# Another order of the operations of chunks 7 and 8 in a fused attention and feed-forward kernel

## The chip, the cores and the metric

The kernel runs on one core of a Trainium2 chip. The metric is the device time of one execution in microseconds (us), the median over several runs. The core's engines are named as in the profile: PE (matrix products; PEld is its weight load), DVE, ACT, POOL and SP. DVE and ACT do elementwise work and read what PE leaves in PSUM; SP, ACT and POOL also issue the transfers (DMAs), each in the order of its own instructions.

## What is computed

Linear attention with cosine and sine weights, then a feed-forward layer with a Swish of its own slope for each column:

```python
q_p = phi(q, cos_w, sin_w)          # relu(x)*cos, relu(x)*sin, side by side
k_p = phi(k, cos_w, sin_w)
kv  = np.einsum('bhsf,bhsd->bhfd', k_p, v)
z   = np.sum(k_p, axis=2)
num = np.einsum('bhsf,bhfd->bhsd', q_p, kv)
den = np.einsum('bhsf,bhf->bhs', q_p, z)[..., None] + 1e-06
x   = (num / den) laid out as 4608 tokens x 512
h   = x @ w_in                      # 512 x 2048
out = (h * sigmoid(beta * h)) @ w_out   # 2048 x 512
```

Batch 8, 8 heads, 576 positions, 64 per head; inputs and output are float32, the products are done in bf16.

## The kernel before

The 4608 tokens are done in nine chunks of 512 (0 to 8). Each chunk's feed-forward part is two large products, and both are done in pairs with seven block products in place of eight (Strassen's scheme): DVE forms sums of input blocks, PE does seven products, and DVE and ACT put the results together in PSUM.

For chunk c there are eight pairs `h0` to `h7` (each gives two column blocks of h) and two pairs `ox` and `oy` of the output. A chunk has four token tiles of 128; pair `ox` makes tiles 0 and 2, pair `oy` tiles 1 and 3. The steps of a pair have one letter each, and `fast_ops` (L455) gives them:

- `1`, `5`, `6`, `2`, `7`, `3`, `4` are the seven products on PE, 2 matmuls each in an `h` pair and 8 in an `o` pair. The digit behind `1` is the PSUM bank of results "b", the digit behind `c` that of results "a".
- `c` (ACT, L471) copies the first product into bank a; `d` (ACT) or `D` (DVE), L475, keeps product 5 in a buffer in SBUF.
- `e` and `f` (DVE, L478) add that buffer to bank b, `e` after product 6 and ahead of 7, `f` after product 7 and ahead of 4. In an `o` pair `f` writes the right half of the second tile into an output buffer, and the kept product and PSUM are its inputs.
- `A` and `B` end the pair. In an `h` pair they are ACT's activation (L416) of bank a (after product 3) and bank b (after product 4). In an `o` pair `A` copies bank a, which is the whole first tile (L648), and `B` the left half of the second (L651), both on ACT; `X` and `Y` are the same copies on DVE, and `U`, `V` (L642) copy the halves of the first tile apart, on DVE.

`s` is one DVE sum of activations for the output products (L406), `t` one of the chunk's inputs (L446), `x` the division that ends the attention of three position blocks. Output buffers come from a pool of four and are taken in the order of the code; the buffers of `d` and `D` come from three names with two each, also in that order.

The order of all this is written out by hand: `ORDERS` holds a string of operations for each chunk, `7/` in the string of chunk 8 marks an operation that belongs to chunk 7, and the code issues them in this order. Each engine then runs its own share strictly in turn and waits where an input is not there yet.

Each finished tile, or half, is stored at once by `store` (L523). For the last chunk the issuing engine depends on the tile: both halves of tile 0 (the copy `oxA`) go by POOL, tiles 1 and 3 (pair `oy`) by SP for one half of the rows and by ACT for the other, tile 2 (`oxf` and `oxB`) by SP and POOL:

```python
own = (nc.sync if c < NTC - 1 else nc.gpsimd if tt == 0 else (nc.sync, nc.scalar if tt % 2 else nc.gpsimd)[hf])
```

In the last chunk's pair `oy` the second tile is stored in halves (`last`, in `o_pair`): the right half as part of `oyf`, the left half as part of `oyY`. So the ACT engine's instruction list holds, beside its copies, the store issues that belong to `oyU`, `oyf`, `oyV` and `oyY`.

Of the kernel before, what the change touches and what calls it, by code (L numbers as in the profile page):

```python
# [22 lines left out]
def kernel(  # L23
# [827 lines left out]
    def w_out_sum(kind):  # L851
# [73 lines left out]
            "oxB oy4 oyV oyY"),  # L925
    }

    pairs, parts = {}, {}
# [111 lines left out]
```

## Time and profile before

| | us |
|---|---|
| median of 3 runs | 274.17 (273.17 to 275.35) |
| the profiled execution: its own time | 273.7 |
| the profiled execution: span from the first instruction to the last | 271.6 |
| PE busy in the span | 261.2 |
| DVE busy | 229.9 |
| ACT busy | 196.6 |
| POOL busy | 36.2 |

The span is 2.1 us shorter than that execution's own time, and that execution was 0.5 us under the median. In the rows below the first column is the start in us from the span's start, the second the duration, then the engine, the line of the code, the operation, what it writes and reads, and how many instructions a row holds; square brackets give the idle time before it and what ended it. A queue that issues DMAs is marked by a q behind the engine's name (SPq, ACTq). A row with a share of busy time is an average over its stretch.

### The profile page before, as it was taken

How to read it: one execution, taken by the hardware profiler on the slowest of the kernel's cores; microseconds unless marked ns; L12 is line 12 of the kernel's file. 1: busy time of each engine (PE TensorE's matmuls, PEld its weight loads, DVE VectorE, ACT ScalarE, POOL GpSimd, SP SyncE). 2: the span in 40 equal slices, each digit the busy share in tenths (PEclk: the TensorE clock that was granted, in tenths of full speed). 3: DMA queues.
4: the chain of work that ended last, by engine and by line, in shares of the span. 5: the costliest groups of instructions: out<-in, count | busy, mean ns of one | idle time of the engine just before them, and what ended most of it. 6: DMA issues, size and time to landing. Idle time of an engine off the chain costs nothing.

```text
span 271.6 us, 9158 instructions
## 1 busy us (share of the span) xinstructions
PE 261.2 (96%) x3784; PEld 212.3 (78%) x3784; DVE 229.9 (85%) x599; ACT 196.6 (72%) x398; POOL 36.2 (13%) x34
## 2 busy tenths in 40 slices
PE   7699999999999999999999999999999999999991
PEld 6356545556888888888888888888888888888880
DVE  5989999999999998999988988898689879856931
ACT  5778677897788996895799668953993479628710
POOL 1444000000003304200042015000330000000002
PEclk9999999999999999999999999999999999999999
DMA  6999999999999999999698878119803241006005
GB/s 239 368 396 382 390 390 304 388 218 360 216 202 329 312 274 229 315 281 234 184 193 257 195 103 246 43 23 119 193 2 64 53 100 33 0 2 156 4 19 135
DMA packets 52441, 54.00 MB, mean 199 GB/s; under 512 B 31232, under 2 KB 31760, under 8 KB 52400
## 3 DMA queue, kind: packets, MB, share of 16 engines
q1 hardware_dynamic: 51904, 52.77, 70.6%
q8 instruction: 29, 0.48, 0.7%
q0 software_dynamic: 144, 0.39, 0.6%
q10 hardware_dynamic: 352, 0.27, 0.4%
q14 instruction: 12, 0.10, 0.1%
HBM read 36.71 MB, written 9.44 MB: 170 GB/s over the span
## 4 chain that ended last, share of the span: by engine, by line
PE 85%; DMA 9%; DVE 2%; issue 1%; ACT 1%; SPq 1%; POOL 0%; ACTq 0%; POOLq 0%
PE ps L611 36%; PE ps L502 32%; PE ps L386 7%; DMA raw_q<-in_q_dram 6%; PE ps L297 4%; DMA raw_k<-in_k_dram 3%; PE ps L276 3%; PE ps L534 3%; DVE xs L319 1%; SPq L79 1%; PE ps L235 0%; PE ps L356 0%; DVE win L115 0%; POOL out_dram L527 0%; DVE qb L193 0%
## 5 line engine op out<-in xcount | busy, mean ns | idle before, releaser
L416 ACT ACTIVATE g_t<-ps,beta 128x512 bf16<-128x512 f32 x112 | 71.3, 691 | 7.0 <-PE ps L502 6.3
L502 PE MATMUL ps<-w_stage 128*128 128x256 bf16 x336 | 56.3, 273 | 0.0
L611 PEld LDWEIGHTS <-S 128*128 128x128 bf16 x512 | 49.6, 98 | 6.4 <-issue 0.4
L502 PEld LDWEIGHTS <-w_stage 128*128 128x128 bf16 x448 | 43.8, 98 | 5.1
L478 DVE TENSOR_TENSOR ps<-ps,p 128x256 f32<-128x256 f32 x85 | 35.9, 429 | 8.4 <-PE ps L502 3.3
L611 PEld LDWEIGHTS <-g_t 128*128 128x128 bf16 x384 | 36.8, 98 | 4.8
L502 PE MATMUL ps<-xt,win 128*128 128x256 bf16 x224 | 39.7, 273 | 0.0
L502 PEld LDWEIGHTS <-win 128*128 128x128 bf16 x336 | 32.6, 98 | 3.9
L611 PE MATMUL ps<-wout,g_t 128*128 128x256 bf16 x256 | 32.4, 273 | 0.0
L471 ACT COPY ps<-ps 128x256 f32<-128x256 f32 x72 | 26.4, 372 | 6.9 <-PE ps L611 3.7
L611 PE MATMUL ps<-wout,S 128*128 128x256 bf16 x256 | 31.1, 273 | 0.0
L611 PE MATMUL ps<-T,S 128*128 128x256 bf16 x256 | 30.9, 273 | 0.2 <-issue 0.2
L223 POOL TENSOR_TENSOR qs<-qt,tanr 128x1152 bf16<-128x1152 bf16 x6 | 14.3, 2389 | 118.7 <-ACT o_sb L648 55.4
L386 PE MATMUL ps<-xt,win 128*128 128x512 bf16 (+1 forms) x156 | 28.5, 341 | 0.1
L406 DVE TENSOR_TENSOR S<-g_t 128x512 bf16<-128x512 bf16 x64 | 25.6, 417 | 1.7 <-ACT g_t L416 1.2
L394 ACT ACTIVATE g_t<-ps,beta 128x512 bf16<-128x512 f32 x32 | 21.1, 690 | 4.9 <-PE ps L386 4.7
L386 PEld LDWEIGHTS <-win 128*128 128x128 bf16 x156 | 15.0, 98 | 11.7 <-issue 0.2
L319 DVE TENSOR_TENSOR xs<-ps,rden 128x768 bf16<-128x768 f32 (+4 forms) x26 | 22.8, 884 | 0.8
L478 DVE TENSOR_TENSOR ps<-ps,u 128x256 f32<-128x256 f32 x43 | 18.5, 429 | 5.1 <-PE ps L502 2.4
L475 ACT COPY p<-ps 128x256 f32<-128x256 f32 x27 | 9.9, 376 | 15.9 <-PE ps L611 11.4
L502 PE MATMUL ps<-xt,w_stage 128*128 128x256 bf16 x112 | 20.7, 273 | 0.0
L502 PE MATMUL ps<-w_stage,win 128*128 128x256 bf16 x112 | 19.8, 273 | 0.0
(99 smaller groups left out, 385.8 us busy)
## 6 DMA issues: line engine op xcount, KB each, us to landing
out_dram<-o_sb SPq DMA_DIRECT2D x65, 128.0 KB, 3.3
raw_v<-in_v_dram SPq DMA_DIRECT2D x7, 1152.0 KB, 7.9
raw_k<-in_k_dram SPq DMA_DIRECT2D x7, 1152.0 KB, 10.9
raw_q<-in_q_dram SPq DMA_DIRECT2D x7, 1152.0 KB, 7.4
w_stage<-in_moe_w_in_dram SPq DMA_DIRECT2D x3, 1024.0 KB, 13.3
w_stage<-in_moe_w_out_dram SPq DMA_DIRECT2D x2, 1024.0 KB, 8.8
w_stage<-in_moe_w_out_dram SPq DMA_DIRECT2D x4, 512.0 KB, 12.0
raw_q<-in_q_dram SPq DMA_DIRECT2D x2, 576.0 KB, 4.7
```

The costliest lines, as they stand in the source:

```text
L223: return eng.tensor_tensor(dst.rearrange("q n (g p) -> q n g p", g=2), src.rearrange("q n (g p) -> q n g p", g=2), tanr[:, n0:n1].unsqueez ...
L297: nc.tensor.matmul(ps[cols, bank + jj, slot * E : (slot + 1) * E], lhsT=(qts[b % 2], qs_of(b))[cs][rows, jp, n, cols], rhs=kv[rows, g, jp, ...
L319: nc.vector.tensor_tensor(o.rearrange("q j n s d -> q j (n s) d"), nv[:, :, a:z, :, 0:D].rearrange("q j n s d -> q j (n s) d"), rden[:, :, ...
L386: nc.tensor.matmul(ps[:, h_bank(c, jt), i * 64 : (i + w) * 64], lhsT=win[jt // 4][:, mi, (jt % 4) * P : (jt % 4 + 1) * P], rhs=xt[:, i : i ...
L394: return nc.scalar.activation(gs[c, jt // 4][:, jt % 4], ps[:, h_bank(c, jt)], AF.Silu, scale=beta[:, jt : jt + 1])
L406: return nc.vector.tensor_tensor(o, l, r, op=op)
L416: return nc.scalar.activation(gs[c, jt // 4][:, jt % 4], bank, AF.Silu, scale=beta[:, jt : jt + 1])
L471: return nc.scalar.copy(at("a", 0), at("b", 0))
L475: return (nc.scalar.copy if eng == "act" else nc.vector.tensor_copy)(st["p5"], at("b", 1))
L478: nc.vector.tensor_tensor(dst, at("b", 0), st["p5"], op=ALU.add)
L502: nc.tensor.matmul(dst, lhsT=l[:, g], rhs=r[:, :, g * HP : (g + 1) * HP], start=start and g == 0, stop=g == 1, skip_group_check=True)
L611: nc.tensor.matmul(dst, lhsT=l(i), rhs=r[:, i], start=start and i == 0, stop=i == order[-1], skip_group_check=True)
```

## The change

Only the strings of chunks 6, 7 and 8 in `ORDERS` differ; no operation is added or left out, but four of them change their engine.

```diff
@@ chunk 6, end
-            "h7B s10 h6B oy10 N25 s12 oyc3 ox14 s13 s23 oy2 s22 oxc7 oy5 ox2"),
+            "h7B s10 h6B oy10 N25 s12 oyc3 ox14 s13 s21 s23 oy2 s22 oxc7 oy5 ox2"),
@@ chunk 7, beginning
-            "h212 6/s20 6/s42 6/oyD 6/ox5 6/s21 6/x2 6/t1 6/s33 6/ox6 6/oy6 h315 h111 6/s30 h15 6/oxd 6/oye h25 6/s32 "
+            "h212 6/s20 6/oyd 6/s42 6/ox5 6/x2 6/t1 6/s33 6/ox6 6/oy6 h111 h315 6/s30 6/s41 h15 6/oxd 6/oye 6/s32 6/s43 "
...
-            "6/s41 h016 6/s40 6/s43 h2d 6/oxe 6/oy7 6/oyf 6/oy3 h1D 6/oyA 6/t2 t1 6/ox3 h35 6/t3 h05 h0D h3D h2c3 6/oy4 "
-            "6/oxA 6/t4 h22 h1c7 h26 6/oyB h2e h16 h1e 6/ox7 h23 t3 h3c0 h17 h27 h12 h13 6/oxf h36 h1f h2f h14 6/ox4 "
+            "h25 6/s40 6/oy7 6/oxe h2d h016 6/oyf 6/oy3 6/t2 6/ox3 h35 t1 6/t3 6/oyA h05 h0D h2c3 6/oy4 h1d 6/oxA h3D "
+            "6/t4 h22 h1c7 h26 h16 6/oyY 6/ox7 h2e h1e h23 t3 h17 h3c0 h27 h13 6/oxf h12 h36 h1f h2f h14 6/ox4 h3e h24 "
...
@@ chunk 8, middle
-            "7/s41 h07 h37 h33 7/oyD 7/oxd 7/s40 h3f h2B 7/oy2 7/oxc2 7/ox6 7/oye 7/ox2 7/s32 h32 7/oy7 7/s43 h3A 7/oxe "
-            "7/ox7 7/ox3 7/oyf 7/oxf 7/ox4 7/oxB h0f h34 7/oxX h02 h510 h112 h04 h3B h15 h1c7 7/oy4 h1D h55 h03 h16 "
+            "7/s41 h37 h07 7/oy2 h33 7/oyD 7/oxd 7/s40 h3f h2B 7/oxc2 7/ox6 7/oye 7/ox2 7/s32 h32 7/oy7 h3A 7/s43 h34 "
+            "7/oxe 7/ox7 7/oxf 7/ox3 7/oyf 7/ox4 7/oxB h0f 7/oxX h02 h510 h112 h04 h3B h15 h1c7 7/oy4 h03 h1D h55 h16 "
...
@@ chunk 8, end
-            "s23 s22 ox5 oyc7 s40 oxd oy5 s33 oy2 s42 s43 oyd s41 ox6 oy6 oxe ox3 oyU ox7 oye oxf oy7 ox4 oyf oxA oy3 "
-            "oxB oy4 oyV oyY"),
+            "ox5 s23 s22 s40 oyc7 oy5 s33 oxd oy2 s42 s43 oyd s41 ox6 oy6 oxe ox3 oyU oye ox7 oxf oy7 ox4 oxA oyf oy3 "
+            "oy4 oxB oyV oyY"),
```

Seen engine by engine, these are all the differences.

- **ACT.** `oyd` of chunk 6, `h1d` of chunk 7 and `h2d` of chunk 8 come to ACT from DVE; `oyB` of chunk 6 goes to DVE as `oyY`. In chunk 8, `h0c5` goes ahead of `h2A`, and chunk 7's `oyB` ahead of `h0A`. At the end `oxA` goes ahead of the store that belongs to `oyf`.
- **DVE.** The same four operations leave or come. Some of the sums change places: `s21` and `s41` of chunk 6 come earlier, `s22` of chunk 7 later, `s21` of chunk 8 earlier and `s31` later. In chunk 7 `oxf` goes ahead of `oyf`, and `h7D` ahead of `s11`.
- **PE.** `h11` and `h31`, `h12` and `h13` of chunk 7 change places; `oy7` of chunk 6 goes ahead of `h01` of chunk 7. In chunk 8, `h05` goes behind `h23` and `h27`, `h37` ahead of `h07`, `h34` from behind chunk 7's `ox4` to ahead of its `ox7`, `h03` ahead of `h55`; chunk 7's `oy2` goes ahead of `h33`.
- **SP and POOL** have the same lists as before.

The end of ACT's list, as a difference (rows that begin with - stand before, with + now). L475 are `oxd` and `oyd`, L527 the issue of a store, L648 is `oxA`, L651 `oxB`:

```order
-L475 COPY p_5203<-ps 128x256
-L475 COPY u<-ps 128x256
-L527 DMA out_dram<-o_sb 64x256 x2
-L648 COPY o_sb<-ps 128x512
+L475 COPY p_5212<-ps 128x256
+L475 COPY u<-ps 128x256
+L527 DMA out_dram<-o_sb 64x256
+L648 COPY o_sb<-ps 128x512
+L527 DMA out_dram<-o_sb 64x256
 L651 COPY o_sb<-ps 128x256
 L527 DMA out_dram<-o_sb 64x256 x2
```

Before, two store issues (of `oyU` and of `oyf`) stood ahead of the copy `oxA`; now one does, and that of `oyf` comes after it.

ACT's list at the beginning of chunk 7, before, from `oyc3` and `oxc7` of chunk 6 on:

```order
214 L471 COPY ps<-ps 128x256 x2
215 L475 COPY p_4586<-ps 128x256
216 L475 COPY p_4597<-ps 128x256
217 L648 COPY o_sb<-ps 128x512
218 L471 COPY ps<-ps 128x256
219 L648 COPY o_sb<-ps 128x512
220 L471 COPY ps<-ps 128x256
221 L651 COPY o_sb<-ps 128x256
222 L471 COPY ps<-ps 128x256
```

and now:

```order
214 L471 COPY ps<-ps 128x256 x2
215 L475 COPY u<-ps 128x256
216 L475 COPY p_4587<-ps 128x256
217 L475 COPY p_4604<-ps 128x256
218 L648 COPY o_sb<-ps 128x512
219 L471 COPY ps<-ps 128x256
220 L475 COPY p_4648<-ps 128x256
221 L648 COPY o_sb<-ps 128x512
222 L471 COPY ps<-ps 128x256 x2
```

The new row 215 is `oyd`, the new row 220 is `h1d`, which stands between `h2c3` (219) and `oxA` (221) with `h1c7` behind that; the L651 copy `oyB` is gone from here.

DVE's list where chunk 7's output pairs end, before:

```order
486 L478 TENSOR_TENSOR ps<-ps,p_4934 128x256
487 L478 TENSOR_TENSOR o_sb<-ps,p_4932 128x256
488 L478 TENSOR_TENSOR o_sb<-ps,p_4934 128x256
489 L478 TENSOR_TENSOR ps<-ps,p_4911 128x256
490 L648 COPY o_sb<-ps 128x512
```

and now:

```order
483 L478 TENSOR_TENSOR ps<-ps,p_4942 128x256
484 L478 TENSOR_TENSOR o_sb<-ps,p_4942 128x256
485 L478 TENSOR_TENSOR o_sb<-ps,p_4940 128x256
486 L478 TENSOR_TENSOR ps<-ps,p_4911 128x256
487 L648 COPY o_sb<-ps 128x512
```

The rows are `oxe`, then before `oyf`, `oxf` and now `oxf`, `oyf` (each known by the kept product that it reads), then `h0f` of chunk 8 and `oxX`.

18 rows, old and new, of the table ORDERS are left out of this document.

## The prediction, made before the changed kernel was run

> **What bounds the kernel now.** I read the page first, then the table by stretches over the part that the change touches, then the order of time at the end, and last the transfers of the end. On the page the span and the engines' busy time stand:
>
> ```profile
> span 271.6 us, 9158 instructions
> PE 261.2 (96%) x3784; PEld 212.3 (78%) x3784; DVE 229.9 (85%) x599; ACT 196.6 (72%) x398; POOL 36.2 (13%) x34
> ```
>
> An average hides whether the changed part has gaps. By stretches (start and end, length, then PE, PEld, DVE, ACT and POOL busy, the granted clock, the DMAs):
>
> ```profile
> 188.00:202.00 14.00, 14.00 (x130) 12.54 (x129) 10.76 (x30) 11.92 (x26) 4.79 (x2) 1.00 0.63 107
> ...
> 244.00:258.00 14.00, 14.00 (x130) 12.55 (x129) 10.64 (x29) 11.08 (x24) 0.00 (x0) 1.00 0.34 77
> 258.00:263.00 5.00, 5.00 (x48) 4.48 (x47) 2.25 (x6) 0.37 (x1) 0.00 (x0) 1.00 0.11 26
> 263.00:265.90 2.90, 2.83 (x26) 2.28 (x24) 0.88 (x3) 0.86 (x2) 0.69 (x1) 1.00 0.18 45
> 265.90:271.60 5.70, 0.00 (x0) 0.00 (x0) 0.39 (x1) 0.00 (x0) 1.06 (x3) 0.91 0.54 138
> ```
>
> From 188 us on PE has no pause until its last product, at the full granted clock: 14.00 of 14.00 us, 5.00 of 5.00. So everything that the change moves inside chunks 6 to 8 can win nothing; it can only make PE wait. The last 5.7 us are another matter: PE is done and only copies, stores and landings are left. There the end is set, and this is how it goes, engine by engine:
>
> ```profile
> 260.43 2.78 PE L611 MATMUL ps<-wout,S 128*128 128x256 bf16 x24
> 263.05 1.04 PE L611 MATMUL ps<-T,g_t 128*128 128x256 bf16 x8
> 264.79 1.04 PE L611 MATMUL ps<-T,g_t 128*128 128x256 bf16 x8
> ...
> 262.37 0.43 DVE L478 TENSOR_TENSOR o_sb<-ps,p 128x256 f32<-128x256 f32 x1 [1.23 <-PE ps L611]
> 263.25 0.42 DVE L478 TENSOR_TENSOR o_sb<-ps,u 128x256 f32<-128x256 f32 x1 [0.45 <-PE ps L611]
> 264.99 0.42 DVE L642 COPY o_sb<-ps 128x256 f32<-128x256 f32 x1 [1.32 <-PE ps L611]
> 265.87 0.42 DVE L651 COPY o_sb<-ps 128x256 f32<-128x256 f32 x1 [0.45 <-PE ps L611]
> ...
> 263.70 0.50 ACTq L527 DMA_DIRECT2D out_dram<-o_sb  x1
> 264.32 0.59 ACT L648 COPY o_sb<-ps 128x512 f32<-128x512 f32 x1 [5.94 <-PE ps L611]
> 264.80 0.38 ACT L651 COPY o_sb<-ps 128x256 f32<-128x256 f32 x1
> ```
>
> The 24 matmuls from 260.43 are `ox3`, `ox7` and `oy7`, then come `ox4` (263.05), `oy3` and `oy4` (264.79). DVE does `oxf`, `oyf`, `oyV`, `oyY`, each as soon as its product is there. ACT does not: it stands idle for 5.94 us and starts `oxA` at 264.32, though `ox3` was complete after its 8 matmuls, at about 260.43 + 1.04 = 261.5. The row above tells why. ACT's list holds the issue of `oyf`'s store ahead of `oxA`; it waits for `oyf` (263.25 + 0.42 = 263.67) and occupies ACT's list from 263.70 to 264.20. The profile's chain of waits takes the same way, DVE, then ACT's issue, then the copies:
>
> ```profile
> 263.25 0.43 DVE o_sb L478
> ...
> 263.70 0.50 ACTq L527
> ...
> 264.80 0.39 ACT o_sb L651
> ```
>
> The stores follow, and they come in one heap:
>
> ```profile
> 265.20 0.47 SPq L527 DMA_DIRECT2D out_dram<-o_sb  x1
> 265.21 0.71 POOL L527 DMA_DIRECT2D out_dram<-o_sb  x1 [64.52 <-ACT o_sb L651]
> 265.45 0.47 ACTq L527 DMA_DIRECT2D out_dram<-o_sb  x1
> 265.76 0.55 SPq L527 DMA_DIRECT2D out_dram<-o_sb  x1
> 265.92 1.04 POOL L527 DMA_DIRECT2D out_dram<-o_sb  x2
> 266.32 0.49 ACTq L527 DMA_DIRECT2D out_dram<-o_sb  x1
> 266.40 0.94 SPq L527 DMA_DIRECT2D out_dram<-o_sb  x1
> ```
>
> **The end, worked out.** The stores' time from issue to landing (queue, count, KB each, median us): first the two pairs that are alone (`oyU`, `oyf`), then those of the heap, then the two last (`oyY`).
>
> ```profile
> out_dram<-o_sb SPq DMA_DIRECT2D x2, 64.0 KB, 1.9
> out_dram<-o_sb ACTq DMA_DIRECT2D x2, 64.0 KB, 2.2
> ...
> out_dram<-o_sb POOLq DMA_DIRECT2D x3, 128.0 KB, 3.6
> out_dram<-o_sb SPq DMA_DIRECT2D x1, 128.0 KB, 2.3
> ...
> out_dram<-o_sb ACTq DMA_DIRECT2D x1, 64.0 KB, 4.1
> out_dram<-o_sb SPq DMA_DIRECT2D x1, 64.0 KB, 4.2
> ```
>
> The last store is issued at 266.40 and lands 4.2 us later, at 270.6; the span ends 1.0 us after that, at 271.6. A 64 KB store that takes about 2 us alone takes twice that behind the heap: 640 KB (`oxA` 256, `oxB` 256, `oyV` 128) were issued in the 1.2 us ahead of it.
>
> With the change, step by step:
>
> - `oxA` starts when `ox3` is there: 261.5, and ends at 262.1 (0.59). POOL's two issues follow from 262.1 (0.71, then 0.53, half of the row with two), done by 263.4. Behind the copy in ACT's list stands `oyf`'s store, not due until 263.70: no cost.
> - `oxB` needs `ox4` (263.05 + 1.04 = 264.1) and ACT's free list (264.20, then the 0.12 to the next copy that the rows show now): 264.32 in place of 264.80. Its stores go at 264.7: SP's 0.5 us earlier, POOL's, which stands third in POOL's list, 1.7 us earlier (it is the second of the row from 265.92 now, at about 266.44).
> - `oyV` is bound to PE (264.99). SP's issue for it now waits for SP's issue for `oxB`; it comes at 265.44 in place of 265.76.
> - `oyY` is bound to PE too: 265.87 + 0.42, so both its issues go at 266.32, SP's 0.08 earlier than now.
>
> So the last landing is 266.32 + L, the end 1.0 later. L has no row of its own. Its lower end is the lone 1.9 to 2.2, its upper end the present 4.2. In proportion to what is in the way, with ACT's rows (2.2 alone, 4.1 behind 640 KB, so 1.9 for 640): only `oyV`'s 128 KB ahead gives 2.2 + 0.4 = 2.6; `oxB`'s 256 KB still in the way as well gives 2.2 + 1.1 = 3.3. `oxB`'s stores are issued 1.6 us ahead of `oyY`'s and SP's of that size landed in 2.3, so most of them is through: I take 2.6. The end is 266.32 + 2.6 + 1.0 = 269.9, **1.7 us** earlier. The bounds: 2.4 us (L 1.9), 1.0 us (L 3.3), 0.1 us (L 4.2).
>
> The Trainium skill, page "DMA: Bandwidth & Descriptors", section "Anatomy of one DMA — SWDGE (gpsimd) path", has a fit of 2.0 us plus the bytes over 436 GB/s for one DMA. As an estimate from that page, 64 KB would take 2.15 us and `oyY` would land as if alone, a gain of 2.1. The lone rows, 1.9 and 2.2, agree with it; the heap's 4.1 and 4.2 do not.
>
> **The moves inside chunks 6 to 8.** Three 0.42 us copies leave DVE and one comes; ACT gets three and loses one. Neither engine ends the kernel, so the sums cost nothing unless PE meets a late operand. The closest of these places are two. First ACT in chunk 7 (`h2c3`, `oxA`, `h1c7`) and PE's use of the last, `h16`, which is the third of the four matmuls (0.109 apart: 264.79 less 263.05 over 16):
>
> ```profile
> 215.40 0.36 ACT L471 COPY ps<-ps 128x256 f32<-128x256 f32 x1
> 215.66 0.59 ACT L648 COPY o_sb<-ps 128x512 f32<-128x512 f32 x1
> 216.29 0.36 ACT L471 COPY ps<-ps 128x256 f32<-128x256 f32 x1
> ...
> 216.98 0.60 PE L502 MATMUL ps<-w_stage 128*128 128x256 bf16 x4
> ```
>
> `h1d` in between pushes `oxA` and `h1c7` back by 0.26 (the step from the first row to the second) to 0.37. `h1c7` then ends between 216.9 and 217.0, `h16` is due at 217.2: 0.2 to 0.3 us are left of 0.55. That is about what suffices now at the end, where `oxf` ends at 262.80 and `ox4` follows at 263.05 without a pause. Second, DVE at the end of chunk 7, `oxf` and `oxX`, and PE's `h11` of chunk 8, which is the fifth of the six matmuls and takes over the bank that `oxX` reads:
>
> ```profile
> 241.63 0.42 DVE L478 TENSOR_TENSOR o_sb<-ps,p 128x256 f32<-128x256 f32 x1 [0.45 <-PE ps L611]
> 242.50 0.69 DVE L648 COPY o_sb<-ps 128x512 f32<-128x512 f32 x1
> ...
> 243.40 0.82 PE L502 MATMUL ps<-xt,win 128*128 128x256 bf16 x6
> ```
>
> `h34`, two matmuls, now stands ahead of `ox7`, so `oxf` comes 0.22 later, at 241.85, and `oyf`, `h0f` and `oxX` queue behind it in steps of some 0.34. `oxX` ends at 241.85 + 3 x 0.34 + 0.69 = 243.6, `h11` is due at 243.40 + 4 x 0.109 = 243.84: 0.27 left of 0.65. I cost both at nothing, hidden by that slack; if it is too short, PE stops for 0.1 to 0.4 us at each, and with no later gap to take it up the end moves by as much. The other moves leave more by the trace, so I cost them at nothing too; rival 3 has what is missed here. A gain below the row of PE is excluded, since PE has no pause to lose.
>
> **The rivals.**
>
> 1. *The last store lands as if alone* (L 1.9 to 2.2). For it: the lone pairs, and `oxA`'s 256 KB gone by then (262.8 + 3.6 = 266.4). Against: `oyV`'s stores still go 0.9 us ahead. Gain 2.1 to 2.4: 271.8 to 272.1.
> 2. *The heap only changes its members.* `oxB`, `oyV` and `oyY` still go within 1.6 us, and with L of 3.3 to 4.2 the gain is 1.0 to 0.1: 273.2 to 274.1. For it: POOL's transfers are the slow ones (3.6), and one of them still goes only 1.6 us ahead of the last store. Against: SP's 128 KB store in the midst of the heap landed in 2.3.
> 3. *PE stops in chunk 7 or 8* for 0.3 to 1.5 us in all, at the places above or at one that I did not see: 272.8 to 274.0. For it: slacks of 0.2 to 0.3. Against: the same slack works all along the present end.
> 4. *Slower: POOL's issues get in DVE's way.* They move from 265.2 to 262.1, onto `oxf` (262.37), which PE's `ox4` needs at 263.05. If `oxf` had to wait until POOL's stores have landed (262.8 + 3.6 = 266.4) it would be 4.0 late, `ox4` and all behind it 3.8 (0.25 slack): 274.2 - 1.7 + 3.8 = 276.3. If only until POOL's issues are done (263.4), it costs 0.75 and stays a gain. It decides from a wait of 1.95 us on. Against it: `oyV` and `oyY` ran beside POOL's issues now (264.99 beside 265.21, 265.87 beside 265.92) and took 0.42, as `oyf` did without them.
>
> On rival 4 the Trainium skill, page "SBUF — State Buffer", section "Who interferes with whom", says that a DVE instruction with at most one input in SBUF and outside the two-port modes does not contend with POOL. By that rule `oxf`, with one input in PSUM, is safe; the two copies agree with it, and no row shows such a sum beside POOL's issue.
>
> **How the numbers follow.** The sum is made on the profiled execution (273.7, span 271.6): 272.0. It ran 0.5 us under the median of 274.17; on that scale the forecast is 274.17 - 1.7 = 272.5. Chances: forecast (L near 2.6, PE without a pause) 0.45, rival 1 0.25, rival 2 0.14, rival 3 0.10, rival 4 0.04, anything else 0.02. The range goes from rival 1 with half a us for the scatter of medians, 271.3, to the upper end of rival 2, 274.2. One per cent, about what a measurement can tell from no change, is 2.7 us, more than the whole end can give (2.4): faster by over 1% only with scatter on top of rival 1, 0.07; slower by over 1% needs 276.9, beyond rival 4, 0.03; within 0.90.
>
> **What would show it.** Right: ACT's 512-wide copy at 261.5, POOL's first issue near 262.1 and its third near 264.7, PE still full from 188 us on, the last SP and ACT issues at 266.3 and landing in 2.2 to 3.3 us. Wrong: a pause of PE anywhere after 205 us, `oxf` longer than 0.43 or late beside POOL's issue, or last stores that still take over 4 us.

## The result and the profile after

| | us |
|---|---|
| before, median of 4 runs | 274.57 (273.17 to 275.35) |
| changed, median of 4 runs | 271.44 (270.62 to 271.64) |
| ratio, 95% interval | 0.9886 (0.9838 to 0.9934) |
| the changed kernel's profiled execution: own time, span | 271.64, 269.6 |

The forecast was 272.5, the range 271.3 to 274.2. The first comparison gives 3.1 us; the two profiled spans differ by 2.0 (271.6 to 269.6). Beside the experiments below, on one chip, the changed kernel had 272.16 against 273.79 of before: ratio 0.9931 (0.9911 to 0.9951). The two intervals overlap, and 2.0 us (0.73%) lies in both, so I take the larger first figure for scatter of few runs; that was not tested by itself.

In the table by stretches of the changed kernel (start and end, length, PE, PEld, DVE, ACT, POOL, clock, busy share of the DMA engines, GB/s that they moved) PE is as full as before, and the piece behind it is shorter:

```profile
202.00:216.00 14.00, 14.00 (x259) 12.26 (x258) 12.00 (x34) 6.11 (x15) 0.00 (x0) 1.00 0.27 45
216.00:230.00 14.00, 14.00 (x131) 12.54 (x130) 11.69 (x32) 11.66 (x25) 0.00 (x0) 1.00 0.34 77
230.00:244.00 14.00, 14.00 (x131) 12.55 (x129) 9.40 (x26) 6.26 (x15) 0.00 (x0) 1.00 0.01 1
244.00:258.00 14.00, 14.00 (x131) 12.55 (x129) 10.46 (x28) 11.24 (x24) 0.00 (x0) 1.00 0.33 77
...
265.90:269.60 3.70, 0.00 (x0) 0.00 (x0) 0.42 (x1) 0.00 (x0) 0.00 (x0) 1.00 0.50 138
```

The end of the changed kernel in order of time:

```profile
261.53 0.59 ACT L648 COPY o_sb<-ps 128x512 f32<-128x512 f32 x1 [3.12 <-PE ps L611]
262.40 0.42 DVE L478 TENSOR_TENSOR o_sb<-ps,p 128x256 f32<-128x256 f32 x1 [1.23 <-PE ps L611]
262.42 1.24 POOL L527 DMA_DIRECT2D out_dram<-o_sb  x2 [61.71 <-ACT o_sb L648]
...
263.73 0.50 ACTq L527 DMA_DIRECT2D out_dram<-o_sb  x1
...
264.33 0.37 ACT L651 COPY o_sb<-ps 128x256 f32<-128x256 f32 x1 [2.21 <-PE ps L611]
...
264.82 1.04 PE L611 MATMUL ps<-T,g_t 128*128 128x256 bf16 x8
264.99 0.52 POOL L527 DMA_DIRECT2D out_dram<-o_sb  x1 [1.33 <-ACT o_sb L651]
...
265.89 0.42 DVE L651 COPY o_sb<-ps 128x256 f32<-128x256 f32 x1 [0.45 <-PE ps L611]
```

ACT now does `oxA` as soon as PE has it, at 261.53 in place of 264.32, POOL stores it from 262.42, and the issue for `oyf` (263.73) comes behind. PE ends where it did (264.82 + 1.04 = 265.86, before 265.83), and `oyY` starts at the same time. The two last stores, issued at 266.35, take half of the 4.2 and 4.1 us that they took before (queue, count, KB, us to landing):

```profile
out_dram<-o_sb SPq DMA_DIRECT2D x1, 64.0 KB, 1.9
out_dram<-o_sb ACTq DMA_DIRECT2D x1, 64.0 KB, 2.2
```

The chain of waits from 262 us on no longer goes through ACT's queue. Up to the last copy it is PE, then `oyY`, and nothing else (the landing behind it is not in this view):

```profile
261.93 3.94 PE ps L611 x36
265.87 0.02 issue
265.89 0.42 DVE o_sb L651
```

A good measure for the experiments is the time from the end of PE's last matmul group to the end of the span, since it leaves out by how much an execution started sooner or later: 271.6 - 265.83 = 5.8 us before, 269.6 - 265.86 = 3.7 us now. The difference of the two is 2.0 us before rounding (5.77 - 3.74).

### The profile page after: what moved, and what is told of

It is laid out like the page before. It is cut to its first block, busy times and chain, and to the rows that moved or that the text cites. A ratio compares the mean times of both kernels' runs of the same rounds, so it can differ in the third digit from the quotient of the medians.

```text
span 269.6 us, 9150 instructions
## 1 busy us (share of the span) xinstructions
PE 261.7 (97%) x3780; PEld 213.4 (79%) x3784; DVE 229.3 (85%) x597; ACT 197.2 (73%) x400; POOL 36.3 (13%) x34
## 4 chain that ended last, share of the span: by engine, by line
PE 84%; DMA 12%; DVE 2%; SPq 1%; issue 0%
PE ps L611 37%; PE ps L502 32%; DMA raw_q<-in_q_dram 7%; PE ps L386 5%; DMA w_stage<-in_moe_w_in_dram 5%; PE ps L297 4%; PE ps L534 3%; PE ps L276 2%; DVE win L115 1%; SPq L79 1%; PE ps L235 0%; PE ps L356 0%; DVE qb L193 0%; DVE o_sb L651 0%; SPq L101 0%
## 5 line engine op out<-in xcount | busy, mean ns | idle before, releaser
L475 ACT COPY p<-ps 128x256 f32<-128x256 f32 x29 | 10.7, 376 | 14.7 <-PE ps L611 10.0
```

Of the source, the lines that this page charges most:

```text
L475: return (nc.scalar.copy if eng == "act" else nc.vector.tensor_copy)(st["p5"], at("b", 1))
```

## The experiments

Seven runs, one of them the changed kernel again, on two chips. In all ratios the kernel before was run beside them. The diffs of the order show the end of chunk 8's string alone, joined into one line.

**One move alone.** Only `oxA` ahead of `oyf` in the kernel before:

```diff
-ox4 oyf oxA oy3 oxB oy4 oyV oyY
+ox4 oxA oyf oy3 oxB oy4 oyV oyY
```

> The kernel before with one move alone: oxA ahead of oyf at the end of chunk 8. My theory (the whole gain is at the end: oyf's store issue kept ACT from oxA) expects the end of the changed kernel: oxA at 261.5, the last SP and ACT stores issued at 266.3 to 266.4 and landing in 1.9 to 2.4 us, span 269.4 to 269.8, ratio to before 0.988 to 0.994. The rival (some of the gain comes from the moves inside chunks 6 to 8, since the medians differ by 3.1 us and the end gives only 2.0) expects a ratio of 0.995 or more, about 1 us behind the changed kernel.

Measured: 271.74 against 273.79, ratio 0.9923 (0.9902 to 0.9943), span 269.6. Its end is that of the changed kernel, to a few hundredths:

```profile
261.54 0.58 ACT L648 COPY o_sb<-ps 128x512 f32<-128x512 f32 x1 [3.12 <-PE ps L611]
263.74 0.50 ACTq L527 DMA_DIRECT2D out_dram<-o_sb  x1
264.34 0.37 ACT L651 COPY o_sb<-ps 128x256 f32<-128x256 f32 x1 [2.21 <-PE ps L611]
```

PE ends at 265.87, so 3.7 us to the end. This one move is the whole gain, as far as these runs can tell.

**All but that move.** The changed kernel with `oyf` ahead of `oxA` again:

```diff
-ox4 oxA oyf oy3 oy4 oxB oyV oyY
+ox4 oyf oxA oy3 oy4 oxB oyV oyY
```

> The changed kernel with that one move undone: oyf ahead of oxA again, everything else of the change kept. My theory expects the end of before: oxA near 264.3, ACT idle some 6 us ahead of it, last landings after 4 us or more, span 271.4 to 271.8, ratio 0.997 to 1.003. The rival expects a ratio of 0.993 to 0.997, the rest of the 3.1 us. If the other moves cost PE time that the end hides, the ratio is above 1.002 and PE shows a pause after 205 us.

Measured: 273.82 against 273.79, ratio 0.9986 (0.9966 to 1.0006). The old picture is back, ACT's 5.94 us included:

```profile
264.77 0.58 ACT L648 COPY o_sb<-ps 128x512 f32<-128x512 f32 x1 [5.94 <-PE ps L611]
265.25 0.38 ACT L651 COPY o_sb<-ps 128x256 f32<-128x256 f32 x1
```

The span, 272.1, is above what I wrote, but this execution reached PE's end 0.46 us later from its start on (265.25 + 1.04 = 266.29); the piece behind it is 5.8 us, that of before. All other moves of the change together are worth nothing that these runs can tell. (They include one that the list of differences above leaves out: on DVE, `s43` of chunk 6 now stands ahead of `s40`.)

**The change once more**, beside these two:

> The changed kernel once more, beside the other two on one chip. My theory expects it equal to the kernel with the one move alone, within 0.3% (ratio to before 0.988 to 0.994). The rival expects it 0.3 to 0.5% faster than that one.

Measured: 272.16, ratio 0.9931 (0.9911 to 0.9951), as the one move alone (271.74, 0.9923); the rival, which wanted it 0.3 to 0.5% ahead of that, falls. Its profiled execution has a span of 269.0 and PE's end at 264.27 + 1.04 = 265.31, so again 3.7 us.

**The wait made longer.** The kernel before, with `oxA` and `oxB` behind the store of `oyV` as well:

```diff
-ox4 oyf oxA oy3 oxB oy4 oyV oyY
+ox4 oyf oy3 oy4 oyV oxA oxB oyY
```

> The kernel before with the suspected wait made longer: oxA and oxB behind the store issue of oyV too, so ACT can't copy them before about 266.0. If the place of oxA in ACT's list sets the end, oxA starts near 266.0 (1.7 later than before), POOL's first issue near 267 and its last near 268.5, last landings 3 to 4 us later, span 272.6 to 273.6, ratio 1.003 to 1.008. If the end is bound by oyY and its two stores whatever ACT does (rival), the span stays within 0.4 us of 271.6.

Measured: 274.49 against 273.79, ratio 1.0024 (1.0012 to 1.0036), span 272.4 with PE's end at 264.63 + 1.04 = 265.67, so 6.7 us behind it in place of 5.8. The direction is as expected, the size below it by a little: the span was to be 272.6 or more.

```profile
265.91 0.59 ACT L648 COPY o_sb<-ps 128x512 f32<-128x512 f32 x1 [7.69 <-DMA out_dram<-o_sb]
266.17 0.51 ACTq L527 DMA_DIRECT2D out_dram<-o_sb  x1
266.39 0.38 ACT L651 COPY o_sb<-ps 128x256 f32<-128x256 f32 x1
```

`oxA` came where it was expected (265.91), but one of `oyY`'s stores left at 266.17, ahead of the heap, and POOL's last landed 3.2 us after its issue in place of 4.0.

**The block taken out, the order kept.** The kernel before, but both parts of `oyf`'s store are issued by SP:

```diff
         if last:
-            store(c, pr + 2, sb["2"], half * HM, (half + 1) * HM)
+            store(c, pr + 2, sb["2"], half * HM, (half + 1) * HM, nc.sync if half else None)
```

> The kernel before, its order kept, but both halves of the rows of oyf's store are issued by SP, so ACT's list holds no wait for oyf ahead of oxA. If that queued issue is the cause, oxA starts at 261.5 and POOL's first issue is at about 262.4, without any change of order: span 269.4 to 270.0, ratio 0.988 to 0.994. If it is rather the order of the output buffers or of the semaphores that changed with the order (rival), oxA stays near 264.3 and the span near 271.6.

Measured: 271.87 against 274.10, ratio 0.9916 (0.9893 to 0.9938), span 269.4.

```profile
261.34 0.58 ACT L648 COPY o_sb<-ps 128x512 f32<-128x512 f32 x1 [3.12 <-PE ps L611]
263.96 0.37 ACT L651 COPY o_sb<-ps 128x256 f32<-128x256 f32 x1 [2.04 <-PE ps L611]
265.29 1.37 ACTq L527 DMA_DIRECT2D out_dram<-o_sb  x2
```

With PE's end at 265.67 these are again 3.7 us, and no operation changed its place. So it is the store issue in ACT's list that held `oxA`, and not which buffers or semaphores an order brings with it.

**Early copy, late stores.** The changed kernel, with `oxA`'s stores issued behind those of `oxB`:

```diff
                 got = copy(sb_tile("1"), bank("a"))
-                store(c, pr, sb["1"])
+                if not (c == NTC - 1 and pr == 0):
+                    store(c, pr, sb["1"])
...
                 got = copy(sb["2"][:, 0:HM], at("b", 0))
                 stored(0)
+                if c == NTC - 1 and pr == 0:
+                    store(c, pr, sb["1"])
```

> The changed kernel, oxA copied early as there, but its two stores stand behind oxB's store in POOL's list. Told apart: does the early copy count, or the early stores? If the heap of stores at the end is what makes the last ones land late, POOL issues from about 265.0 to 266.8, the last landings take 3 to 4.2 us in place of 1.9 to 2.2, and the span is 270.4 to 271.5 (1 to 2 us more than the changed kernel). If it is enough that ACT and SP are free (rival), the last SP and ACT stores land in 2.2 and the end moves only as far as POOL's own last store, issued at 266.1 and landing in 2.6: span 269.7 to 270.0.

Measured: 273.18 against 274.10, ratio 0.9964 (0.9950 to 0.9977), span 270.9 and PE's end at 264.81 + 1.04 = 265.85: 5.1 us (5.05 before rounding). The copies are early (261.51, 264.31), and yet the last stores are late again:

```profile
out_dram<-o_sb POOLq DMA_DIRECT2D x1, 128.0 KB, 3.4
out_dram<-o_sb SPq DMA_DIRECT2D x1, 64.0 KB, 3.4
out_dram<-o_sb ACTq DMA_DIRECT2D x1, 64.0 KB, 3.6
```

That a free ACT is enough falls: 1.3 of the 2.0 us hang on the two stores of `oxA` being out of the way.

**Late copies, no stores.** The kernel before without the two stores of `oxA`; 128 tokens of the output are not written:

```diff
                 got = copy(sb_tile("1"), bank("a"))
-                store(c, pr, sb["1"])
+                if not (c == NTC - 1 and pr == 0):
+                    store(c, pr, sb["1"])
```

> The kernel before without the two stores of oxA (token tile 0 of the last chunk, 256 KB, is not stored); the late copies oxA and oxB stay at 264.3 and 264.8. If the heap is the cause of the late landings, 256 KB less at the same late time shorten oyY's landing from 4.2 to 2.2 to 2.8 us: span 269.6 to 270.3, nearly the whole gain though oxA is as late as before. If the late copies hold the end by themselves (through oxB's store and SP's list), the span stays above 270.8.

Measured: 272.24 against 274.10, ratio 0.9935 (0.9912 to 0.9959), span 270.1, PE's end at 264.95 + 1.04 = 265.99: 4.1 us. (L652 is the copy `oxB`; the edit moves it down by a line.)

```profile
264.47 0.58 ACT L648 COPY o_sb<-ps 128x512 f32<-128x512 f32 x1 [5.94 <-PE ps L611]
264.95 0.38 ACT L652 COPY o_sb<-ps 128x256 f32<-128x256 f32 x1
```

```profile
out_dram<-o_sb ACTq DMA_DIRECT2D x1, 64.0 KB, 2.5
out_dram<-o_sb SPq DMA_DIRECT2D x1, 64.0 KB, 2.6
```

ACT is held as long as before, and still 1.7 of the 2.0 us are won. So the late copies hold the end for the most part through the stores that they put in front of `oyY`'s. The edit does a second thing: `oxB`'s store is now first in POOL's list and goes at 265.63 in place of 266.44. What each of the two is worth was not told apart.

## Why the prediction was right, step by step

*PE has no pause to lose, so nothing inside the chunks can win.* Right: all but the one move gives 0.9986 (0.9966 to 1.0006), and PE's rows are full before and after, 14.00 of 14.00 us in each stretch from 188 to 258.

*ACT waits for `oyf`'s store issue, and `oxA` can start at 261.5.* Right, at 261.53, and shown twice: by the order and, with the order kept, by another queue for the issue.

*POOL's issues follow at 262.1.* Off by 0.3: POOL issued at 262.42, 0.30 after the copy's end (261.53 + 0.59), and at 264.99, 0.29 after `oxB`. The rows of before show the same step, which the prediction overlooked: `oxA` ended at 264.32 + 0.59 = 264.91, POOL's first issue is at 265.21. SP's issue follows its copy by 0.02 there (`oxB` ended at 265.18, SP's issue is at 265.20). The error cost nothing here.

*The landing of the last stores, L.* This is the term that was mis-sized. I took L = 2.6 in proportion to the bytes in front, with the bound 1.9 to 4.2; it was 2.2, that of a store alone. So the span ended at 269.6 in place of the 269.9 that I worked out, and the end gave 2.0 us in place of 1.7. Rival 1 had this landing; I gave it 0.25. The first median, 271.44, lies only 0.1 above the lower end of the range, which reaches that far by the half us for scatter; the second, 272.16, lies between rival 1 (271.8 to 272.1) and the forecast.

What failed is the proportion. Four kernels show L of `oyY`'s store on ACT by what is issued in front of it, and how long before:

| in front of it | issued in the last 1.6 us | issued in the last 1.1 us |
|---|---|---|
| 384 KB (`oxB`, `oyV`) | 2.2 (changed) | 2.5 (no stores of `oxA`) |
| 640 KB (`oxA` too) | 3.6 (early copy, late stores) | 4.1 (before; 128 of the 640 KB just behind) |

The 640 KB of the prediction were not all in front: POOL's third store, 128 KB, goes at 266.44, just behind both of `oyY`'s (266.32 and 266.40). 384 KB delay ACT's store by 0.0 to 0.3 us over the 2.2 of a store alone; the next 256 KB by 1.4 to 1.6 more. Why bytes in front cost so unevenly can be read from when they move. Two stretches of before, then two of the changed kernel (the last number is GB/s):

```profile
265.50:266.30 0.80, 0.33 (x4) 0.05 (x1) 0.42 (x1) 0.00 (x0) 0.80 (x2) 1.00 0.01 1
266.30:270.00 3.70, 0.00 (x0) 0.00 (x0) 0.00 (x0) 0.00 (x0) 0.66 (x2) 1.00 0.82 213
```

```profile
265.50:266.30 0.80, 0.36 (x4) 0.07 (x1) 0.41 (x1) 0.00 (x0) 0.01 (x1) 1.00 0.66 149
266.30:268.20 1.90, 0.00 (x0) 0.00 (x0) 0.02 (x1) 0.00 (x0) 0.00 (x0) 1.00 0.78 228
```

Before, next to nothing moves from 265.5 to 266.3, though the heap's first stores were issued from 265.20 on. Then all of it, `oyY`'s 128 KB included, moves until 270.0: 213 x 3.7 = 0.79 MB. In the changed kernel the DMA engines are already at work, 228 x 1.9 = 0.43 MB are left at 266.3, and they are through by 268.2. The rate is much the same, so what differs is how many bytes are left when the last stores are issued. As an estimate, the 0.36 MB more take 1.6 us at 228 GB/s, most of the 1.9 by which ACT's last landing differs (4.1 and 2.2). That bytes in front cost nothing while they are through before the last store's own bytes can move is my reading of these rows; no run varied the bytes by themselves.

The Trainium skill, page "DMA: Bandwidth & Descriptors", section "Anatomy of one DMA — SWDGE (gpsimd) path", has the fit from which the prediction worked out an estimate of 2.15 us for 64 KB. The changed kernel's last landings, 1.9 and 2.2, lie on either side of it; before's 4.1 and 4.2 do not fit it. The section's fit is for one DMA on POOL's path, while these stores are issued by SP and ACT and have others in front. The same page, section "Issuing engines are not separate DMA queues", says that transfers issued by SP, ACT and POOL run on the same 16 DMA engines and interleave. That the removal of two stores of POOL brings the last store of ACT from 4.1 to 2.5 agrees with it.

*The close places in chunks 7 and 8.* Right; both slacks sufficed. In the changed kernel `h1d` pushed ACT's `oxA` and `h1c7` back by 0.30, and PE's group of four starts on time:

```profile
215.69 0.38 ACT L475 COPY p<-ps 128x256 f32<-128x256 f32 x1
215.96 0.60 ACT L648 COPY o_sb<-ps 128x512 f32<-128x512 f32 x1
216.59 0.36 ACT L471 COPY ps<-ps 128x256 f32<-128x256 f32 x1
```

`h1c7` ends at 216.95, and the third matmul of PE's group, which starts at 217.00, comes at 217.22. At the end of chunk 7 DVE's `oxX` ends at 242.88 + 0.68 = 243.56, as worked out (243.6), and PE's `h11` at 243.86 is not held up:

```profile
242.88 0.68 DVE L648 COPY o_sb<-ps 128x512 f32<-128x512 f32 x1
...
243.42 0.82 PE L502 MATMUL ps<-xt,win 128*128 128x256 bf16 x6
```

*Rival 2 (the heap only changes its members)* fell: L was 2.2. *Rival 3 (PE stops)* fell with the full rows. *Rival 4 (POOL's issue in DVE's way)* fell too: `oxf` started at 262.40, within 0.02 us of POOL's issue at 262.42, and took 0.42, and `ox4` was not late.

No version that might beat both kernels was tried: behind PE's end there are now `oyY` (0.42), the landing of a store alone (2.2) and the 1.0 us of the end. I see no order of the same operations that shortens these, but that is not shown.

## What to carry to other kernels

A store that a compute engine issues stands in that engine's list and waits there for its data; whatever compute stands behind it waits as well, so put it behind copies that are ready sooner, or give it to a queue with no compute. At the end of a kernel look at the landing times of the last stores in the profile: where they are twice those of a store alone, look at which bytes have not moved yet when these stores are issued, and get those out earlier. Where the bounding engine shows no pause in a stretch, moves there can be costed at nothing or at a loss, and the gain sought behind its last instruction.

## What the runs showed of the hardware that was not expected

- POOL's store issues start 0.29 to 0.30 us after the copy that they wait for, in the changed kernel twice; SP's and ACT's start 0.02 to 0.04 after theirs. The first of POOL's three issues took 0.71 us and the others 0.52 to 0.53.
- Two 64 KB stores that SP and ACT issue in the same moment, with nothing else under way (the pair of `oyU`), do not land together: SP's takes 1.9, ACT's 2.2, before and in the changed kernel. In the last pair, with other stores under way, it can be the other way round, as in the kernel with `oyf`'s store on SP:

```profile
out_dram<-o_sb SPq DMA_DIRECT2D x1, 64.0 KB, 2.2
out_dram<-o_sb ACTq DMA_DIRECT2D x1, 64.0 KB, 2.0
```

- The time at which PE ends varies by 1.0 us between executions of nearly the same order (265.31 to 266.29 in the numbers above, 265.31 and 265.86 for the changed kernel alone), with no pause of PE from 188 us on; the piece behind it repeats within 0.1 us for the same order of the end. Why the earlier part scatters was not tried.
